# A gated window-attention decode kernel: the load of w_in issued as 16 rows and then 112 rows

## The chip, the cores and the metric

The kernel runs on one core of a Trainium2 chip. The metric is device time in microseconds (us) of one launch; the kernel before takes 217.18 us, the median of three runs (216.87 to 217.79). The profile beside it is one execution recorded by the hardware profiler. All tensors are float32.

## What is computed

One decode step for two sequences: window attention over the last 4096 positions of a key and value cache, times a gate that a small gated MLP makes from the same normalised input.

```python
x = A_x                                   # [2, 1, 512]
xn = _layernorm(x, axis=-1)
# s: q = xn @ wq (32 heads of 128), softmax over the last W = 4096 of 32768 cached keys,
#    8 key/value heads, 4 query heads on each, then @ wo (4096 x 512)
s = _A_ref(xn, A_k_cache, A_v_cache, A_wq, A_wo)
# g: z = gelu(xn @ w_in) (512 x 1792), half of it normalised and mixed, then @ w_out (896 x 512)
g = _silu(_B_ref(xn, B_w_in, B_w_sp, B_b_sp, B_w_out))
return x + s * g
```

The arithmetic is small, since two rows of input meet every weight and every cached key once. The bytes are not: w_in has 3.67 MB, w_out 1.84, wq 8.39, wo 8.39, and the eight heads' windows of keys and values 67.1 MB, 89.4 MB in all, each read once from device memory (HBM).

## The kernel before

**Tiles.** Each large load fills one tile of 128 partitions in the on-chip memory SBUF. The tile `win` (line 95) holds w_in with 7168 numbers, 28,672 bytes, to a partition: partition p gets four neighbouring rows of w_in, which lie together in HBM, so a partition's share is one unbroken piece. `wout` holds 14,336 bytes to a partition, and each of the two `wq` tiles, the eight K tiles and the eight V tiles 32,768.

**The ring.** `win`, the two `wq` tiles, all K and V tiles and the two `wo` tiles share a ring of four slots (`slot`, lines 85 and 86); `wout` has a place of its own. A load into a slot waits until the tile that was there has been used: k1, the fifth tile of the ring, goes where `win` was, v0 where the first `wq` tile was, and so on.

**Queues.** All large loads are issued by SyncE (SP) in program order: `win` (line 96), `wout` (98), two of `wq` (103), then K and V heads in turn (120), then `wo` in eight pieces. One issue writes descriptors for the core's 16 DMA engines, and these work through them on their own. ScalarE issues three tiny loads (`xs`, the two rows of x, at line 93, and the scalars w_sp and b_sp) and the store of the result; GpSimd issues one small load of x.

**Who waits.** TensorE starts with the product `z` = xn @ w_in, whose 16 matmuls need all of `win`. The queries need `wq`; then each head's keys are transposed by VectorE, scored by TensorE, made into probabilities and multiplied with the values. At the end `wo` is multiplied in, and one store writes the result. Every compute engine issues in the order of the program text (`InOrder`). Each DMA reports its end on one of eight semaphores that its queue's DMAs take in turn (DMAHW0 to DMAHW7, SP's and ScalarE's loads together); a DMA that comes eight places later takes the same one, and waits until the first has ended.

Of the kernel before, what the change touches and what calls it, by code (L numbers as in the profile page):

```python
# [42 lines left out]
def kernel(  # L43
# [14 lines left out]
    pe, dve, act, sp = (InOrder(tc, e) for e in (nc.tensor, nc.vector, nc.scalar, nc.sync))  # L58
# [26 lines left out]
    def slot(name, *shape):  # L85
        return ring.tile([P, *shape], F32, tag="slot", name=name)
# [6 lines left out]
    act.dma_start(xs, x[:, 0, :])  # L93
    win_v = w_in.rearrange("(p k) f -> p k f", p=P)
    win = slot("win", KT, F)
    sp.dma_start(win, win_v)
    wout = big.tile([P, FT, D], F32, tag="wout", name="wout")
    sp.dma_start(wout, w_out.rearrange("(p j) d -> p j d", p=P))
    wq_v = wq.rearrange("(p k) f -> p k f", p=P)
# [494 lines left out]
```

## Time and profile before

| | us |
|---|---|
| time of the runs, median of 3 | 217.18 |
| profiled execution, first to last instruction (span) | 214.9 |
| `win`: from issue to landing | 11.2 |
| `wout`: from issue to landing | 15.0 |
| TensorE busy | 138.0 |
| VectorE busy | 104.9 |

The profile gives no time of its own for the profiled execution beyond its span; the runs' median is 2.28 us more than the span, for what lies before the first and behind the last instruction. In the rows below, SPq, ACTq and the like are an engine's queue of DMA issues, PEld is TensorE's weight load, DVE VectorE, ACT ScalarE and POOL GpSimd. Nearly every row has line 37, the helper that keeps the program's order, so tiles are told apart by name. A DMA packet in the profile is the transfer of one piece; "share" is the mean busy share of the 16 DMA engines, where a packet is put down whole to the moment at which it starts, so that a short stretch can show more than 1.

### The profile page before, as it was taken

Reading aid. Unit: us, or ns where it says so; the run is one execution under the profiler, and the core shown is the slowest. Engines: PE = TensorE matmul, PEld = TensorE weight load, DVE = VectorE, ACT = ScalarE, POOL = GpSimd, SP = SyncE. Lnnn points to the kernel's source line nnn. Section 1 sums busy time; section 2 is a strip of 40 time slices with the busy share of each in tenths; the row PEclk is TensorE's granted clock in tenths of the full one; section 3 lists DMA queues with packets and bytes.
Section 4 is the critical chain, followed back from the end, with each engine's and each line's share of the span. In section 5 each row is a group of like instructions: output and inputs, shape, how many; then the busy total and the mean of one; then the engine's idle time right before and its main releaser. Section 6 shows DMA issues by size and latency. Waiting matters only on the chain.

```text
span 214.9 us, 2108 instructions
## 1 busy us (share of the span) xinstructions
PE 138.0 (64%) x862; PEld 43.4 (20%) x862; DVE 104.9 (49%) x161; ACT 23.9 (11%) x60; POOL 4.0 (2%) x20
## 2 busy tenths in 40 slices
PE   0172193835865983992594199089467759989873
PEld 0120021212111221220121023033111113432321
DVE  2604014079549549529608910985784387240301
ACT  5003003110001011021021002012100011030110
POOL 7000000000000000000000000000000000000000
PEclk9997578896597698599599559959966757996998
DMA  7999999999999999999999999999999999999990
GB/s 257 428 439 445 433 433 445 401 451 415 451 427 427 442 415 451 409 457 421 439 430 433 445 415 445 415 451 424 421 451 421 451 409 450 415 418 418 427 401 36
DMA packets 4092, 89.52 MB, mean 417 GB/s; under 512 B 486, under 2 KB 498, under 8 KB 884
## 3 DMA queue, kind: packets, MB, share of 16 engines
q1 hardware_dynamic: 4032, 89.39, 96.9%
q8 instruction: 6, 0.10, 0.2%
q14 instruction: 2, 0.02, 0.0%
q10 hardware_dynamic: 20, 0.01, 0.0%
q0 software_dynamic: 32, 0.00, 0.0%
HBM read 89.40 MB, written 0.00 MB: 416 GB/s over the span
## 4 chain that ended last, share of the span: by engine, by line
DMA 69%; DVE 14%; PE 12%; ACT 1%; issue 1%; SPq 1%; ACTq 0%; DVEq 0%
DMA k<-in_A_k_cache_dram 33%; DMA v<-in_A_v_cache_dram 27%; DVE kt L37 11%; DMA wo<-in_A_wo_dram 9%; PE acc L37 5%; PE s L37 4%; PE pp L37 2%; ACT p L37 1%; DVE pT L37 1%; SPq L37 1%; DVE sm L37 1%; DVE qw L37 1%; DVE res L37 0%; PE so L37 0%; DVE mg L37 0%
## 5 line engine op out<-in xcount | busy, mean ns | idle before, releaser
L37 DVE STREAM_TRANSPOSE kt<-k 128x2048 f32<-128x2048 f32 x32 | 72.5, 2285 | 1.4 <-DMA k<-in_A_k_cache_dram 1.3
L37 PE MATMUL acc<-v,pT 128*32 128x512 f32 x256 | 42.6, 825 | 11.6 <-DMA v<-in_A_v_cache_dram 10.2
L37 PE MATMUL s<-kt,qw 128*32 128x512 f32 x256 | 40.3, 683 | 5.7 <-DVE kt L37 4.2
L37 PE MATMUL pp<-p,swap 128*128 128x512 f32 x16 | 12.6, 880 | 20.0 <-ACT p L37 20.0
L37 DVE CUSTOM_DVE_ANT_1 sm<-s,own 128x512 f32<-128x512 f32 x8 | 5.5, 691 | 35.8 <-PE s L37 35.7
L37 PEld LDWEIGHTS acc<-v,pT 128*32 128x32 f32 x256 | 10.7, 156 | 42.1 <-issue 32.0
L37 PE MATMUL q_ps<-wq,xnT 128*32 128x512 f32 x64 | 10.5, 785 | 12.0 <-DMA wq<-in_A_wq_dram 12.0
L37 PEld LDWEIGHTS s<-kt,qw 128*32 128x32 f32 x256 | 10.6, 121 | 33.8 <-issue 19.5
L37 ACT ACTIVATE o<-acc,diag 128x128 f32<-128x128 f32 x30 | 8.7, 367 | 62.6 <-PE acc L37 62.2
L37 ACT ACTIVATE p<-sm,nb 128x512 f32<-128x512 f32 x8 | 5.8, 722 | 77.8 <-DVE nb L37 77.8
L37 PE MATMUL col<-o,selw 128*32 128x128 f32 (+1 forms) x28 | 7.6, 439 | 0.9 <-DVE o L37 0.9
L37 DVE TENSOR_TENSOR lsum<-pl,diag 128x4 f32<-128x4 f32 x3 | 0.5, 162 | 15.7 <-PE pl L37 15.7
L37 PE MATMUL z<-win,xnT 128*32 128x448 f32 x32 | 5.0, 794 | 4.5 <-DMA win<-in_B_w_in_dram 4.5
L37 DVE STREAM_TRANSPOSE pT<-pp 128x512 f32<-128x512 f32 x8 | 5.7, 713 | 4.3 <-PE pp L37 4.3
L37 PEld LDWEIGHTS pp<-p,swap 128*128 128x128 f32 x16 | 3.0, 235 | 20.7 <-ACT p L37 20.7
L37 PE MATMUL mo<-mg,same 128*128 128x16 f32 x16 | 3.2, 273 | 5.8 <-DVE mg L37 5.3
L37 PE MATMUL part<-wo,oT 128*32 128x512 f32 x48 | 5.9, 598 | 0.1
L37 ACT ACT_TABLE_LOAD x4 | 5.1, 1283 | 2.0 <-issue 1.9
L37 PEld LDWEIGHTS q_ps<-wq,xnT 128*32 128x32 f32 x64 | 2.0, 126 | 15.5 <-DMA wq<-in_A_wq_dram 12.2
L37 PE MATMUL xnT_ps<-ident,xn 2*128 2x2 f32 x4 | 0.6, 252 | 6.9 <-DVE xn L37 6.9
L37 PEld LDWEIGHTS mo<-mg,same 128*128 128x128 f32 x16 | 2.4, 188 | 12.2 <-DVE mg L37 12.2
L37 DVE STREAM_TRANSPOSE zt<-z 128x448 f32<-128x448 f32 x1 | 1.0, 978 | 7.8 <-ACT z L37 7.8
(110 smaller groups left out, 62.4 us busy)
## 6 DMA issues: line engine op xcount, KB each, us to landing
k<-in_A_k_cache_dram SPq DMA_DIRECT2D x8, 4096.0 KB, 23.6
v<-in_A_v_cache_dram SPq DMA_DIRECT2D x8, 4096.0 KB, 31.4
wq<-in_A_wq_dram SPq DMA_DIRECT2D x2, 4096.0 KB, 28.8
wo<-in_A_wo_dram SPq DMA_DIRECT2D x2, 2048.0 KB
win<-in_B_w_in_dram SPq DMA_DIRECT2D x1, 3584.0 KB, 11.2
wo<-in_A_wo_dram SPq DMA_DIRECT2D x3, 1024.0 KB, 21.2
wout<-in_B_w_out_dram SPq DMA_DIRECT2D x1, 1792.0 KB, 15.0
wo<-in_A_wo_dram SPq DMA_DIRECT2D x1, 512.0 KB, 25.3
```

What stands on the lines that cost most here:

```text
L37: return self.tc.keep_in_program_order(call(*args, **kwargs))
```

## The change

The one load of `win` becomes two loads of the same tile, issued one after the other: partitions 0 to 15 first, then partitions 16 to 127. Nothing else in the program text is changed.

```diff
     win = slot("win", KT, F)
-    sp.dma_start(win, win_v)
+    FIRST = 16
+    sp.dma_start(win[:FIRST], win_v[:FIRST])
+    sp.dma_start(win[FIRST:], win_v[FIRST:])
     wout = big.tile([P, FT, D], F32, tag="wout", name="wout")
```

On SP, at the start of the program, these are the issues and what each waits for (a number behind a tile's name counts tiles: k_89 is k0, k_91 is k1, v_93 is v0). Before:

```order
L37 DMA win<-in_B_w_in_dram 128x7168
L37 DMA wout<-in_B_w_out_dram 128x3584
L37 DMA wq_79<-in_A_wq_dram 128x8192
L37 DMA wq_81<-in_A_wq_dram 128x8192
L37 DMA k_89<-in_A_k_cache_dram 128x1x8192
L37 DMA k_91<-in_A_k_cache_dram 128x1x8192 [waits DMAHW1_49,DMAHW0_49,PE_49]
L37 DMA v_93<-in_A_v_cache_dram 128x1x8192 [waits DMAHW5_49,PE_49]
```

And of the change, in the same place (k_90 is k0 here, k_92 is k1, v_94 is v0):

```order
L37 DMA win<-in_B_w_in_dram 16x7168
L37 DMA win<-in_B_w_in_dram 112x7168
L37 DMA wout<-in_B_w_out_dram 128x3584
L37 DMA wq_80<-in_A_wq_dram 128x8192
L37 DMA wq_82<-in_A_wq_dram 128x8192
L37 DMA k_90<-in_A_k_cache_dram 128x1x8192 [waits DMAHW0_49]
L37 DMA k_92<-in_A_k_cache_dram 128x1x8192 [waits DMAHW4_49,DMAHW1_49,PE_49]
L37 DMA v_94<-in_A_v_cache_dram 128x1x8192 [waits DMAHW6_49,DMAHW2_49,PE_49]
```

Every issue from `wout` on has one more ahead of it and takes the next semaphore. So k0, the ninth load in all, now takes the semaphore of `xs` (DMAHW0) and waits for it; k1 waits for both parts of `win`.

On TensorE, the rows around the first use of `win` read as follows, before (-) and of the change (+):

```order
-L37 MATMUL z<-win,xnT 32x448 [waits DMAHW1_49,DVE_49]
+L37 MATMUL z<-win,xnT 32x448 [waits DMAHW4_49,DMAHW1_49,DVE_49]
 L37 MATMUL z<-win,xnT 32x448 x15
-L37 MATMUL wb_ps<-wb_83,ones 128x2 [waits DMAHW3_49,DMAHW2_49,Pool_49]
-L37 MATMUL q_ps_202<-wq_79,xnT 32x512 [waits DMAHW5_49]
```

No matmul is moved; the first one of `z` waits for two landings where it waited for one.

## The prediction

> **What bounds the kernel now.** I read the page's head and DMA rows first, then the chain that ended last, then the start of the stream in fine slices.
>
> ```profile
> span 214.9 us, 2108 instructions
> PE 138.0 (64%) x862; PEld 43.4 (20%) x862; DVE 104.9 (49%) x161; ACT 23.9 (11%) x60; POOL 4.0 (2%) x20
> ...
> DMA  7999999999999999999999999999999999999990
> ...
> q1 hardware_dynamic: 4032, 89.39, 96.9%
> ...
> DMA 69%; DVE 14%; PE 12%; ACT 1%; issue 1%; SPq 1%; ACTq 0%; DVEq 0%
> ```
>
> No compute engine is busy for more than 64% of the span, while the 16 DMA engines are at nine tenths or more in every slice but the first and the last. SP's queue (q1) alone takes 96.9% of 16 engines' span. The last chain is mostly DMA. The same in stretches, with DMA share and GB/s as the two last columns:
>
> ```profile
> 1.70:2.80 1.10, 0.00 (x0) 0.00 (x0) 0.40 (x2) 0.89 (x1) 1.01 (x6) 1.00 1.48 417
> 2.80:10.80 8.00, 0.61 (x4) 0.55 (x4) 4.15 (x20) 2.08 (x4) 2.05 (x10) 1.00 0.94 402
> 10.80:45.00 34.20, 19.03 (x125) 5.29 (x126) 8.16 (x34) 5.24 (x9) 0.00 (x0) 0.80 1.01 436
> 45.00:90.00 45.00, 30.11 (x146) 8.49 (x150) 31.37 (x28) 2.77 (x8) 0.00 (x0) 0.74 1.00 431
> 90.00:135.00 45.00, 29.91 (x188) 8.88 (x180) 21.48 (x22) 5.05 (x16) 0.00 (x0) 0.80 1.00 433
> 135.00:180.00 45.00, 29.97 (x134) 9.06 (x138) 31.52 (x33) 3.58 (x10) 0.00 (x0) 0.73 1.00 432
> ```
>
> From 10.8 us on the share is 1.00 and the rate stays at 431 to 436 GB/s, whatever is loaded. That is 27 GB/s for each of 16 engines, so that one 28,672-byte piece of `win` takes 28,672 / 27.0 = 1.06 us on its engine. There is no pause in which a late engine could catch up, and the end hangs on the stream:
>
> ```profile
> 191.50 19.59 DMA wo<-in_A_wo_dram
> 211.09 0.04 issue
> 211.13 0.47 PE so L37 x8
> ```
>
> The last piece of `wo` lands at 211.1 us, and 3.8 us of matmul, VectorE and store follow. So **whatever the slowest DMA engine loses or gains in the first transfers moves the end by the same amount.** What matters is the time at which that engine is through with `win`.
>
> Is there really always a next transfer queued? The fifth load of the ring is the first that waits:
>
> ```profile
> 12.03 5.04 PE L37 MATMUL z<-win,xnT 128*32 128x448 f32 x32 [4.50 <-DMA win<-in_B_w_in_dram]
> ...
> 17.13 0.54 SPq L37 DMA_DIRECT2D k<-in_A_k_cache_dram  x1
> ```
>
> It goes out at 17.13, when `z` has done with `win` (12.03 + 5.04 = 17.07). Ahead of it the stream then has `win`, `wout`, two of `wq` and k0: 18.1 MB, 42 us at 432 GB/s, work until 44 us. So `win` may land over 20 us later without starving the stream. The same sum at each later issue in the timeline of SP leaves the least at this one:
>
> ```profile
> 72.80 0.53 SPq L37 DMA_DIRECT2D k<-in_A_k_cache_dram  x1
> ```
>
> There 34.9 MB are queued ahead (those 18.1 and four tiles of 4.19), work until 1.7 + 34.9 / 0.432 = 83 us: 10 us of cover. Those issues wait on landings and on what uses them, so they move together with the stream.
>
> **The start of the stream today.** Slices of 0.2 us; one 28,672-byte piece started in a slice reads 143:
>
> ```profile
> GB/s 0 0 0 0 0 0 0 0 451 860 430 143 287 143 0 0 143 1004 573 143 430 0 573 860 430 430 0 292 860 727 143 292 0 1004 574 287 430 0 573 717
> ```
>
> The first 16 pieces (3, 6, 3, 1, 2, 1) start between 1.6 and 2.8 us, and the second 16 (1, 7, 4, 1, 3) between 3.2 and 4.2. From one piece's start to the next that is some 1.6 us (share 1.48 x 1.10 us x 16 / 16 pieces = 1.63), against 1.06 later. This start-up is all that the change can win: by 10.8 us the stream has moved 417 x 1.1 + 402 x 8.0 = 3675 KB, and 432 GB/s from 1.7 us on would have been 3931, 256 KB or 0.59 us more. The last engine, at its second piece at 4.1, could win a little more.
>
> **The change, part by part.**
>
> *One more issue on SP.*
>
> ```profile
> 0.74 0.37 SPq L37 DMA_DIRECT2D win<-in_B_w_in_dram  x1
> 1.17 0.42 SPq L37 DMA_DIRECT2D wout<-in_B_w_out_dram  x1
> 1.64 1.05 SPq L37 DMA_DIRECT2D wq<-in_A_wq_dram  x2
> 2.74 14.93 SPq L37 DMA_DIRECT2D k<-in_A_k_cache_dram  x2
> ```
>
> It costs about 0.43 us on SP (1.17 - 0.74), and pushes `wout`, `wq` and k0 back by that. Cost 0: `wout` is needed by the DMA engines only after `win`, at about 10 us, and its descriptors go out by 2.1 instead of 1.6. The 112-row issue, from 1.17, reaches the engines 1.0 us later as the first one did (0.74 to 1.7), at 2.2 to 3.2, and the earliest end of a first piece is 1.7 + 1.06 = 2.8: the last engines might wait 0.4 us for it, which is part of the uncertainty below.
>
> *The new waits.* k0's wait for `xs` costs 0, since VectorE reads `xs` at 2.69 us and k0 would be issued at about 3.1 (2.74 + 0.4):
>
> ```profile
> 2.69 0.67 DVE L37 BATCH_NORM_STATS2 st<-xs 2x6 f32<-2x512 f32 x1
> ```
>
> Were `xs` late, the second `wq`, 20 us away in the stream, would cover it. The second landing that `z` and k1 wait for has the cover of 20 us named above.
>
> *The 16-row transfer.* Here lies the decision. Today each of the 16 engines carries 8 of 128 rows, and together they keep 16 times one engine's rate. The trace can't say whether that limit sits in the engine or in the way into SBUF; it shows no large transfer to a few neighbouring rows. If the limit is the engine's own, 16 neighbouring rows go as fast as any: 1.06 us, or 1.63 with today's start-up. If it is the way's, then 16 ways serve 128 rows, eight each. Sixteen neighbouring rows could then lie on as few as two ways, where the pieces take turns: 8 x 1.06 = 8.5 us. Between 1.06 and 8.5 I take 4 turns on four ways, which is the middle in ratio: 4 x 1.06 = 4.25 us. From 1.7 us that ends at 6.0 to 6.2 with the spread of starts, and today the last engine is through with its first piece at 4.1. **Term one: 2.0 us lost**, with -0.9 (the last second piece at 3.2) and 8.5 + 1.7 - 4.1 = +6.1 as ends.
>
> [...]
>
> *The 112-row transfer.* Seven rows to an engine take 7 x 1.06 = 7.4 us if nothing collides, and then win and loss are only term one's. If ways are shared, most ways (12 of 16 with four taken by the first rows) still have all their eight rows to take, at least 8.5 us: +1.1. And blocks of seven rows no longer fit ways of eight: engines meet on a way while others stand empty. If they meet two by two all along, it takes 14.9 us: +7.4. I take the middle, (1.1 + 7.4) / 2. **Term two: 4.2 us lost**, with ends 0 and 7.4. Afterwards, with 128-row transfers, nobody collides, but nothing is caught up either.
>
> **Sum:** 214.9 + 2.0 + 4.2 = 221.1 us of span. The median of the runs lies 2.28 above the span, and nothing in that is touched: 223.4 us.
>
> **The rivals.**
>
> *Nothing is shared: the forecast's opposite side.* With one descriptor to each engine in the first issue, all 16 start close together, and the second issue is there when they are through. The price is the start-up of the row of slices: at most 0.9 us for the last engine, likely half of it. For it: the starts spread over 1.2 us, and the share of 0.94 up to 10.8. Against: the second issue comes 0.43 us behind, and the first pieces take 1.6 us even on engines that start at once, which fewer descriptors don't explain. It decides if 16 neighbouring rows are written at the full 432 GB/s. Time: 217.18 - 0.5 = 216.7, from 216.3 to 217.3.
>
> *Only the first part is slow.* The 112 rows are dealt so that each engine keeps to one way: term two falls to 1.1 or less. For it: today's 128 rows are clearly dealt without collisions, at 1.00 share. Against: 112 / 16 = 7 doesn't divide groups of eight. Time: 217.18 + 2.0 + 1.0 = 220.2.
>
> *The deal is bad.* If the 112 rows go to the engines one by one in turn, 16 neighbours are written at every step: 7 x 4.25 = 29.8 instead of 7.4, +22. And if the change doesn't do what it says and the 16 rows go to one engine, that engine needs 16 x 1.06 = 17 us, +15. Either way 232 to 242. Against: the trace shows no deal of rows among engines at all, only equal shares in the end.
>
> [...]
>
> **Numbers.** Forecast 0.52; only the first part slow 0.17; nothing shared 0.24; bad deal 0.07. Neighbouring rows sharing something is likelier than not, since the stream's rate is the same for four kinds of source with pieces of 14 to 32 KB, which speaks for a limit at the receiving end. I call 0.5%, 1.09 us, what a measurement can tell from no change. "Nothing shared" lies within it, but for a little on the fast side: faster 0.03, same 0.22, slower 0.75. The range reaches from 216.4 to 217.18 + 10 = 227.2, which is the forecast with term two at its end and term one at 2.6; beyond lie the bad deal and a small part of the two-way case. The forecast's own range is 219.5 to 227.2.
>
> **What would show it.** In the fine slices, the second 16 pieces start at about 6 us rather than 3.2 to 4.2; if they start by 3.4, "nothing shared" holds. `win` lands at 16 to 19 us rather than 12, and the rate from 2.8 to 10.8 falls well under 402 GB/s; if it lands by 14 with the first pieces slow, the 112 rows were dealt well. From 20 us on the rate should be 432 again and each later issue shifted alike, with `wo` landing some 6 us after 211.1. The forecast is wrong if `win` lands by 12, or if the shift is absorbed before the end, which would mean that the stream pauses somewhere after all.

## The result and the profile after

The changed kernel takes 224.81 us (median of 6 runs, 224.62 to 225.25) against 217.55 for the kernel before beside it: 7.26 us more, a ratio of 1.0342 with a 95% interval of 1.0321 to 1.0364. It is slower, as forecast, and 1.4 us slower than the 223.4 predicted.

The page's head, slices, q1 row and chain, of the changed kernel:

```profile
span 222.9 us, 2109 instructions
PE 134.5 (60%) x862; PEld 42.5 (19%) x862; DVE 105.0 (47%) x161; ACT 23.9 (11%) x60; POOL 4.0 (2%) x20
...
DMA  9898999999999999999999999999999999999990
GB/s 165 232 257 327 466 429 429 453 393 453 435 418 459 400 450 435 418 465 394 453 432 418 465 394 453 435 418 462 400 447 435 423 459 404 435 412 435 412 381 17
...
q1 hardware_dynamic: 4048, 89.39, 96.8%
...
DMA 67%; PE 15%; DVE 12%; another core or an unknown queue 2%; ACT 1%; SPq 1%; issue 1%; ACTq 0%; DVEq 0%
```

The DMA engines look as busy as before: eights and nines in every slice but the last, 96.8% of the span. Only the row of GB/s gives it away. The first four slices move 165 to 327 GB/s while the engines read as busy: each piece takes longer. By the packets' records the 112 rows' pieces take 1.84 us in the mean, where in the kernel before all pieces of `win` but the first 16 take 1.06. Busy time of a DMA engine is not work done, and here the bytes have to be read beside it.

Stretches of the changed kernel, DMA share and GB/s as the two last columns:

```profile
1.70:18.60 16.90, 0.61 (x4) 0.55 (x4) 4.55 (x21) 2.97 (x4) 3.06 (x14) 1.00 1.02 235
18.60:45.00 26.40, 13.89 (x90) 4.30 (x94) 5.82 (x29) 3.74 (x6) 0.00 (x0) 0.81 1.01 435
45.00:90.00 45.00, 29.16 (x159) 8.62 (x150) 26.84 (x30) 3.70 (x10) 0.00 (x0) 0.77 1.00 430
90.00:135.00 45.00, 28.13 (x158) 8.12 (x162) 28.03 (x22) 4.48 (x14) 0.00 (x0) 0.75 1.00 433
135.00:180.00 45.00, 30.29 (x168) 9.36 (x160) 26.45 (x33) 4.11 (x13) 0.00 (x0) 0.83 1.01 434
```

By 18.6 us the stream has moved 16.9 x 235 = 3972 KB, where 432 GB/s would have moved 7301: it is 7.7 us behind a perfect start, and before it was 0.6. The difference, 7.1 us, is nearly the whole result. From 18.6 us on the rate is that of before, 430 to 435 GB/s, and nothing is caught up.

The loss then goes through the program to its end. First TensorE's product with `win`, then two issues of SP (v0 and k3), then the end of the chain that ended last, all of the changed kernel:

```profile
19.78 5.28 PE L37 MATMUL z<-win,xnT 128*32 128x448 f32 x32 [12.25 <-DMA win<-in_B_w_in_dram]
```

```profile
39.56 0.54 SPq L37 DMA_DIRECT2D v<-in_A_v_cache_dram  x1
...
80.75 0.54 SPq L37 DMA_DIRECT2D k<-in_A_k_cache_dram  x1
```

```profile
199.30 19.55 DMA wo<-in_A_wo_dram
218.85 0.04 issue
218.89 0.47 PE so L37 x8
```

`z` starts 7.75 us later (12.03 before), v0 is issued 7.80 later (31.76 before), k3 7.95 later (72.80 before), and the last piece of `wo` lands 7.76 later (211.09 before). Not every issue moves by the same: the first piece of `wo`, here before and then of the changed kernel, goes out only 6.07 us later.

```profile
181.55 10.28 SPq L37 DMA_DIRECT2D wo<-in_A_wo_dram  x8
```

```profile
187.62 12.00 SPq L37 DMA_DIRECT2D wo<-in_A_wo_dram  x8
```

These two executions lie 8.0 us apart in span (214.9 and 222.9), where the medians of the runs lie 7.26 apart. The profiled execution of the kernel before was a short one: beside the experiments its spans were 215.0 to 216.4 us. So shifts read from the traces come out up to some 0.7 us larger than the result.

### The profile page after: what moved, and what is told of

Its sections match the earlier page's. It is cut to its first block, busy times and chain, and to the rows that moved or that the text cites. A ratio compares the mean times of both kernels' runs of the same rounds, so it can differ in the third digit from the quotient of the medians.

```text
span 222.9 us, 2109 instructions
## 1 busy us (share of the span) xinstructions
PE 134.5 (60%) x862; PEld 42.5 (19%) x862; DVE 105.0 (47%) x161; ACT 23.9 (11%) x60; POOL 4.0 (2%) x20
## 3 DMA queue, kind: packets, MB, share of 16 engines
q1 hardware_dynamic: 4048, 89.39, 96.8%
## 4 chain that ended last, share of the span: by engine, by line
DMA 67%; PE 15%; DVE 12%; another core or an unknown queue 2%; ACT 1%; SPq 1%; issue 1%; ACTq 0%; DVEq 0%
DMA v<-in_A_v_cache_dram 40%; DMA wq<-in_A_wq_dram 18%; DMA wo<-in_A_wo_dram 9%; DVE kt L37 8%; PE acc L37 7%; PE s L37 3%; PE pp L37 2%; PE q_ps L37 1%; DVE gate L37 1%; PE ys L37 1%; SPq L37 1%; ACT p L37 1%; DVE pT L37 1%; DVE sm L37 1%
## 5 line engine op out<-in xcount | busy, mean ns | idle before, releaser
L37 PE MATMUL acc<-v,pT 128*32 128x512 f32 x256 | 39.7, 776 | 11.7 <-DMA v<-in_A_v_cache_dram 10.3
L37 PE MATMUL s<-kt,qw 128*32 128x512 f32 x256 | 39.6, 665 | 4.6 <-DVE kt L37 4.1
L37 PE MATMUL q_ps<-wq,xnT 128*32 128x512 f32 x64 | 9.4, 714 | 11.3 <-DMA wq<-in_A_wq_dram 11.3
L37 PEld LDWEIGHTS s<-kt,qw 128*32 128x32 f32 x256 | 9.4, 120 | 33.6 <-issue 20.5
L37 PEld LDWEIGHTS pp<-p,swap 128*128 128x128 f32 x16 | 2.9, 228 | 20.7 <-ACT p L37 20.7
L37 PE MATMUL qj_ps<-qT,selj 128*128 128x64 f32 x8 | 2.0, 428 | 4.8 <-DVE qT L37 4.8
```

Of the source, the lines that this page charges most:

```text
L37: return self.tc.keep_in_program_order(call(*args, **kwargs))
```

## The experiments

Two theories could explain slow pieces, and two more a late stream. **Shared ways into SBUF:** the partitions written at one time decide the rate. **HBM neighbours:** the places read at one time decide it. **An awkward 112:** the number of rows deals badly. **The start:** few rows in the first transfer, or one more issue ahead of a cold stream, cost the time. Every kernel below loads the same bytes in all and changes only the issues named. "Ways" is a picture: the runs show which partitions slow each other, not what the ways are.

### Where the rate is set: destination or source

Eight transfers of 16 rows take the place of the one load of `win`, in three ways.

```diff
-    sp.dma_start(win, win_v)
+    for s in range(8):
+        sp.dma_start(win[16 * s : 16 * s + 16], win_v[16 * s : 16 * s + 16])
```

> w_in is loaded as eight transfers of 16 neighbouring partitions each, from 16 neighbouring pieces of HBM. Shared ways into SBUF: every transfer has four ways, its pieces take turns four deep, 8 x 4.25 = 34 us for w_in instead of 8.5, the end 20 to 26 us later than before (about 238 to 243 us). Pieces that lie beside each other in HBM as the cause: just as slow. 112 rows being an awkward number for dealing as the cause: no loss, since 16 deals evenly, within 2 us of before.

```diff
-    sp.dma_start(win, win_v)
+    for s in range(8):
+        sp.dma_start(win[s:P:8], win_v[16 * s : 16 * s + 16])
```

> Eight transfers of 16 partitions that lie eight apart (0, 8, .., 120), each from 16 neighbouring pieces of HBM, so the rows of w_in end in other partitions and z is made from mixed rows. Shared ways into SBUF: the partitions reach more ways, with pieces two by two, 8 x 2.1 = 17 us for w_in, the end 7 to 9 us later than before (about 225 us), far from the kernel with neighbouring partitions. HBM neighbours as the cause: the same time as the kernel with neighbouring partitions and the same source. An awkward 112: within 2 us of before.

```diff
-    sp.dma_start(win, win_v)
+    for s in range(8):
+        sp.dma_start(win[16 * s : 16 * s + 16], win_v[s:P:8])
```

> Eight transfers of 16 neighbouring partitions, each from 16 pieces of HBM that lie eight apart; z is made from mixed rows. Shared ways into SBUF: 20 to 26 us later than before, as with neighbouring pieces in HBM. HBM neighbours as the cause: most of the loss gone, within 5 us of before. An awkward 112: within 2 us of before.

| partitions written | pieces read | us | ratio to before (95%) |
|---|---|---|---|
| 16 neighbours | 16 neighbours | 238.90 | 1.0935 (1.0860 to 1.1011) |
| 16, eight apart | 16 neighbours | 225.65 | 1.0329 (1.0257 to 1.0401) |
| 16 neighbours | 16, eight apart | 238.75 | 1.0928 (1.0851 to 1.1006) |

The kernel before took 218.17 us beside them. The source makes no difference (238.90 and 238.75); the destination makes 13 us. With eight issues in each of the three, the number of issues can't be what parts them. Five transfers' time in the middle of the first and the third kernel, then two transfers' time (4.44 us) of the second:

```profile
8.50:28.00 19.50, 0.00 (x0) 0.00 (x0) 1.34 (x8) 0.00 (x0) 0.00 (x0) 1.00 1.01 118
```

```profile
8.50:28.00 19.50, 0.00 (x0) 0.00 (x0) 1.42 (x9) 0.00 (x0) 0.00 (x0) 1.00 1.01 118
```

```profile
12.98:17.42 4.44, 0.00 (x0) 0.00 (x0) 0.00 (x0) 0.00 (x0) 0.00 (x0) 1.00 1.01 207
```

Sixteen neighbouring partitions take 118 GB/s, sixteen that lie eight apart 207, and all 128 take 432. At 118 GB/s the 16 pieces need 458,752 / 118,000 = 3.9 us instead of 1.06: 3.7 turns, where the prediction took four. How the pieces start is seen in the 0.5 us slices of the first 20 us, for the first kernel:

```profile
GB/s 0 0 0 754 172 0 0 0 57 516 344 0 0 0 0 0 57 522 346 0 0 0 0 0 115 516 287 0 0 0 0 0 115 631 172 0 0 0 0 57
```

A burst of 16 pieces starts (754 + 172 = 926 GB/s, x 0.5 us = 463 KB) and then none until the next. By the packets' records the first 16 pieces take 3.0 us in the mean and all later ones 3.9: the pieces go in step, and none runs ahead.

### An awkward 112, the start, and the bytes

Two halves, which deal evenly:

```diff
-    sp.dma_start(win, win_v)
+    sp.dma_start(win[:64], win_v[:64])
+    sp.dma_start(win[64:], win_v[64:])
```

> w_in as two transfers of 64 partitions each, four rows to an engine. Shared ways into SBUF: half of the ways for each transfer, pieces two by two, up to 17 us instead of 8.5, the end 6 to 9 us later than before (about 224 to 226). An awkward 112 or the 16 rows at the start as the cause: no loss, within 1 us of before. HBM neighbours: each engine reads four pieces in a row from its own place as before, so within 1 us of before.

It took 226.38 us against 218.17, 1.0362 (1.0289 to 1.0434): 8.2 us lost. Here two stretches inside `win`'s loading, 8.88 and 4.44 us long, move about half of 432:

```profile
4.10:12.98 8.88, 0.61 (x4) 0.55 (x4) 3.27 (x17) 1.38 (x2) 0.75 (x5) 1.00 1.02 214
12.98:17.42 4.44, 0.00 (x0) 0.00 (x0) 0.00 (x0) 0.00 (x0) 0.00 (x0) 1.00 0.98 200
```

So the loss needs neither 112 rows nor 16. Next, two issues that both span all partitions:

```diff
-    sp.dma_start(win, win_v)
+    sp.dma_start(win[:, :1], win_v[:, :1])
+    sp.dma_start(win[:, 1:], win_v[:, 1:])
```

> w_in as two transfers that both span all 128 partitions: the first quarter of each partition's bytes, then the other three quarters; the same number of issues as the change. Shared ways into SBUF: no loss, since each transfer reaches all ways, 0 to 0.6 us faster than before if the short pieces shorten the start-up, otherwise the same. A second issue at the start as the cause of the loss: 5 us or more slower.

It took 217.29 us against 217.28, 1.0005 (0.9992 to 1.0018): the same. A second issue costs nothing. k0 and k1 have the change's new waits here; `z` has not, since its matmuls on the first part need that part alone and start at 7.86 us. The start of its stream:

```profile
1.70:2.80 1.10, 0.00 (x0) 0.00 (x0) 0.40 (x2) 0.89 (x1) 1.01 (x6) 1.00 0.88 152
2.80:10.80 8.00, 2.33 (x12) 0.75 (x12) 4.15 (x20) 2.08 (x4) 2.05 (x10) 1.00 1.03 439
```

By 10.8 us it has moved 152 x 1.1 + 439 x 8.0 = 3679 KB, and before 3675. Short first pieces don't win the 0.6 us of the start-up back; it only falls in another place.

The split in the running stream, on the second load, with half of the bytes to a partition:

```diff
-    sp.dma_start(wout, w_out.rearrange("(p j) d -> p j d", p=P))
+    wout_v = w_out.rearrange("(p j) d -> p j d", p=P)
+    sp.dma_start(wout[:16], wout_v[:16])
+    sp.dma_start(wout[16:], wout_v[16:])
```

> w_in in one transfer as before; w_out, which comes second and has half the bytes to a partition, as 16 and then 112 partitions, in the running stream. Shared ways into SBUF: the loss goes with the bytes, half of the change's, 3 to 4.5 us later than before. A cause in the start of the stream (the first pieces, cold descriptors): no loss, within 0.5 us of before.

It took 221.30 us against 217.28, 1.0185 (1.0172 to 1.0198): 4.0 us lost, 0.55 of the change's 7.26. Its start, and the stretch in which `wout` is loaded, then that stretch of the kernel before:

```profile
2.80:10.80 8.00, 0.61 (x4) 0.55 (x4) 4.15 (x20) 2.08 (x4) 2.04 (x10) 1.00 0.94 402
10.80:19.00 8.20, 5.60 (x34) 1.76 (x34) 0.00 (x0) 0.11 (x1) 0.00 (x0) 1.00 1.11 268
```

```profile
10.80:19.00 8.20, 5.35 (x34) 1.71 (x34) 1.25 (x4) 0.54 (x1) 0.00 (x0) 1.00 1.04 448
```

The start is that of before (402 GB/s), and the loss comes later (268 GB/s against 448), in a stream that has long been running. So it is no matter of the start. The two transfers in the other order:

```diff
-    sp.dma_start(win, win_v)
+    sp.dma_start(win[16:], win_v[16:])
+    sp.dma_start(win[:16], win_v[:16])
```

> The same two transfers of w_in in the other order: 112 partitions first, then 16. Shared ways into SBUF: about the change's loss, 6 to 8 us later than before, with the 16 pieces now seen in the running stream at three to four times 1.06 us. A cause in the start with few rows: most of the loss gone, within 2 us of before.

It took 226.02 us against 217.28, 1.0400 (1.0383 to 1.0418): 8.7 us lost, 0.7 more than the top of what was expected. The stretch with most of the 16 rows in flight, between the last of the 112 and the first of `wout`, reads

```profile
14.00:17.00 3.00, 0.00 (x0) 0.00 (x0) 0.00 (x0) 0.00 (x0) 0.00 (x0) 1.00 0.98 129
```

not far above the 118 GB/s of neighbours. By the packets' records the last 16 pieces of `win` take 2.7 to 3.8 us each, which is the three to four times 1.06 that was expected. Why this order loses 1.5 us more than the change's stays open; one guess is that there the slow first pieces of the start-up lie under the 16 rows' own slowness, and here they don't.

### How the 112 rows are dealt

The prediction supposed blocks of seven rows to an engine. This kernel is made to force them: seven transfers of 16 partitions, seven apart, give each engine seven neighbours in a row, if the 16 pieces of each transfer go to the 16 engines in the order of the partitions. The trace doesn't say which engine carries which piece.

```diff
-    sp.dma_start(win, win_v)
+    sp.dma_start(win[:16], win_v[:16])
+    for s in range(16, 23):
+        sp.dma_start(win[s:P:7], win_v[s:P:7])
```

> After the same first 16 partitions, the other 112 go out as seven transfers of 16 partitions that lie seven apart (16, 23, .., 121, then 17, 24, .. and so on), so that each engine gets seven neighbouring partitions one after the other by force. If the change's 112 rows are dealt in blocks of seven, this kernel does the same in the same order: within 1 us of the change's loss, 6.3 to 8.3 us later than before, and the pieces show the change's rhythm (1.9, 1.9, 1.7, 1.4, 1.6, 1.9, 1.9 us). If the change's rows are dealt in another way, by ways or one by one, the loss or the rhythm differs.

It took 224.33 us against 217.24, 1.0315 (1.0272 to 1.0359): 7.1 us lost. The page's GB/s row of this kernel, whose slices are nearly as long as the changed kernel's:

```profile
GB/s 166 238 258 331 465 448 406 459 393 448 448 406 465 401 445 436 418 459 401 454 433 418 459 401 448 436 424 451 406 448 430 424 455 409 442 401 433 415 393 27
```

Its first five slices are the changed kernel's to within 3% (165, 232, 257, 327, 466). From the packets' records, counted in sixteens in order of their starts, the mean piece takes 2.5, 1.9, 1.6, 1.6, 1.7, 1.9, 1.8 us in the seven transfers after the first here, and 2.4, 1.9, 1.7, 1.4, 1.7, 1.9, 1.8 in the change. (The expectation had 1.9 for the first of the seven.) Time and rhythm fit blocks of seven; they don't prove them. Other splits have other rows, so the likeness says something; 32 and 96 rows:

```diff
-    sp.dma_start(win, win_v)
+    FIRST = 32
+    sp.dma_start(win[:FIRST], win_v[:FIRST])
+    sp.dma_start(win[FIRST:], win_v[FIRST:])
```

> w_in as 32 and then 96 partitions. Shared ways with blocks of neighbouring rows to an engine: two pieces at 2.2 us on eight ways, then six at 1.8 to 1.9 where engines meet, 15.6 us instead of 8.5, 6 to 8 us later than before. Shared ways with the 96 rows dealt so that each engine keeps to one way: 4.4 + 8.5 us, 4 to 5 us later than before. A cost of the 16 rows alone: no loss here.

```profile
GB/s 180 227 210 303 442 457 411 446 421 416 469 416 428 434 431 446 416 428 457 422 431 422 428 457 422 428 428 437 446 416 428 452 434 427 416 416 428 421 388 34
```

It took 225.38 us against 217.24, 1.0376 (1.0326 to 1.0425): 8.1 us lost, just beyond the 6 to 8 of blocks and far from the 4 to 5 of a deal by ways. The first three slices lie at 180 to 227 GB/s, about half of 432. The pieces of the 96 rows take 1.9 to 2.4 us, 2.1 in the mean, where 1.8 to 1.9 was expected; the kernels with partitions eight apart and with halves have 2.2. So 96 partitions in one transfer went hardly faster than 64, and much slower than three quarters of 432 GB/s, which is 324.

## Why the prediction was right, point by point

**What bounds the kernel.** Right. The stream has no pause, and 7.1 us lost in it by 18.6 us came out as 7.26 at the end. But k3 is not the issue with the least cover. When the first piece of `wo` goes out, at 181.55 us, 81.0 MB are queued ahead, work until 1.7 + 81.0 / 0.432 = 189 us, which is 7.6 us of cover against k3's 10. The prediction also said that each later issue would shift alike, but that one moved by 6.07 us and k3 by 7.95. The stream didn't run dry there (share 0.99 and 424 GB/s from 180 to 211 us in the changed kernel), since the loads ahead of that piece were 7 us late themselves.

**One more issue, and the new waits, at nothing.** Right: the columns kernel has the issue and the waits of k0 and k1, and takes the same time as before (217.29 us against 217.28). That `z` waits for both parts cost nothing either: in the changed kernel it starts at 19.78 us, and the rate from 18.6 to 45 us stays at 435 GB/s.

**The 16 rows.** Right that they are slowed, too large for this place. The fine slices of the changed kernel's first 8 us:

```profile
GB/s 0 0 0 0 0 0 0 0 451 1290 430 0 143 0 0 0 0 0 0 0 143 0 430 0 574 430 430 287 0 0 0 0 0 0 143 287 717 860 287 0
```

Sixteen pieces start together (3, 9, 3, 1), as many as there are engines, so the transfer does what the change says. The starts are even a little closer together, 15 of 16 within 0.6 us where there were 12. The second pieces start between 4.0 and 5.6 us instead of 3.2 to 4.2; the prediction said 6. So term one measures 5.6 - 4.2 = 1.4 us against 2.0 predicted. The size that was off is the four turns: with the 3.7 of the eight transfers, 1.7 + 3.9 = 5.6 us is about when the last second piece starts. That four came so close is luck, as far as the rows of the kernel before go. The prediction calls it the middle in ratio of 1.06 and 8.5 us, but that middle is 3.0 us, 2.8 turns, and would have made term one 0.6 to 0.8 us.

No run shows how many ways there are, or which partitions lie on one: the 16 ways of eight rows, the four turns on four ways and the meeting two by two stay suppositions. What the runs showed is 118 GB/s for 16 neighbours, the same from either source, 207 for 16 partitions eight apart, 200 to 214 for halves of 64, and 432 for all 128.

**The 112 rows.** Right that they lose most, with blocks of seven that fit the runs, and the term that was mis-sized. I took the middle of 1.1 and 7.4, 4.2 us; with 7.1 in all and 1.4 in term one, it measures 5.7. The step that failed is taking the middle. The upper end, 7.4, stood for engines that meet two by two all along, 2.1 us a piece; the kernel with partitions eight apart has 2.2, but no run shows what meets there. The middle comes to 1.66 us a piece, as if many pieces still went at the 1.06 of the kernel before. By the packets' records the 112 pieces take 1.84 us in the mean, and the quickest of them 1.33. So every piece was slowed, and if ways stood empty, that helped no one. Whether all engines met others, or those that met held up the rest, no run tells.

**The rivals.** "Nothing is shared" fell with the start: the time would have been 216.7. "Only the first part is slow" fell too, since the 112 rows lost four times what the 16 did. Of the bad deal, one row in turn to each engine would have cost 3.9 us a step; the eight transfers of 16 neighbours are that deal by hand and lose 20.7 us. Its other half, all 16 rows on one engine, fell with the 16 pieces that start together. The start-up that "nothing is shared" meant to win, 0.6 us, wasn't won by the columns kernel either, though that one moved 439 GB/s from 2.8 us on.

**The numbers.** `win` was to land at 16 to 19 us; its product started at 19.8. The last piece of `wo` was to land some 6 us later, and landed 7.76 later. The predicted time was 1.4 us low: term two was 1.5 low and term one 0.6 high, 0.4 comes from the kernel before, which ran at 217.55 beside the change rather than at 217.18, and 0.1 is rounding and what happens behind 18.6 us.

## What to carry to other kernels

Where the DMA stream is the bound, let each load into SBUF span all 128 partitions: split it by columns, which cost nothing here (217.29 us against 217.28), and not by partitions, which cost 1.9 to 9.4% of this kernel. In this kernel, whose DMA stream never pauses, 7.1 us lost on one early load came out as 7.26 at the end. DMA engines that read as fully busy may be moving little more than a quarter of what they can (share 1.01 at 118 GB/s, where all 128 partitions take 432), so the GB/s row is read beside the share.

## What the runs showed of the hardware that was not expected

The pieces stay in step: with 16 neighbouring partitions, bursts of 16 start every 3.9 us. More partitions in a transfer need not be faster: 96 of them took pieces of 2.1 us, where two halves of 64 took 2.2, and every piece of the 96 rows took at least 1.9. The 112 rows did better, 1.84 us in the mean, but none of their pieces, the quickest at 1.33, came near the 1.06 of a load over all 128. And 16 neighbouring partitions take 118 GB/s, 0.27 of the full rate, a little more than a quarter. No run here tells why.
